# Reordering a seven-product matrix multiplication: even tiles first, half of the sums beside it, weight sums on VectorE

## The chip, the cores and the metric

The kernel runs on one core of a Trainium2 chip. The metric is device time in microseconds (us) of one execution. A profile's span is about 1.7 us shorter than the time of the same run, since it goes from the first to the last instruction. Engines: TensorE (PE; PEld is its weight load), VectorE (DVE), ScalarE (ACT), GpSimd (POOL) and SyncE (SP), which only issues transfers here.

## The reference

```python
# scan: batch 4, heads 8, 768 steps, head_dim 32, state 16, in chunks
y[:, :, sl] = y_intra + y_inter           # decayed scores @ x, and C @ state
# then, on x = y as 3072 x 256:
h = x @ w_in                              # 256 -> 2048
g = h * np.clip(h + 3.0, 0.0, 6.0) / 6.0
return g @ w_out                          # 2048 -> 256
```

## The kernel before

It cuts the 768 steps into six blocks k = 0 to 5 of 128 steps (512 rows over the batch). In each block TensorE makes a first product h (16 tiles f of 128 columns), ScalarE and VectorE turn each tile into gT, and TensorE makes the second product g @ w_out, with the scan of block k + 1 woven between. Block 0 also decodes the weights, which arrive in pieces as 64-bit floats, and uses a plain second product.

```python
r = ffn.tile([P, TB], FP32, name="r", bufs=3)
nc.scalar.activation(r, h, AF.Relu, bias=half, scale=1.0 / 6.0)
nc.vector.scalar_tensor_tensor(
    out=gTs[k][:, f], in0=r, scalar=1.0, in1=h, op0=ALU.min, op1=ALU.mult)
```

From block 1 on the second product uses seven products of quarters instead of eight. Quarters are even and odd tiles (e) by row halves (r); sums of quarters are made by VectorE, four operations for each two pairs of tiles. The sums of w_out's quarters are made once.

```python
js = slice(j0, j0 + 2)
a11, a12, a21, a22 = (g_quarter(k, e, r)[:, js] for r in range(2) for e in range(2))
for o, p_, q_, op in ((s1, a21, a22, ALU.add), (s2, s1, a11, ALU.subtract),
                      (a21, a11, a21, ALU.subtract), (s4, a12, s2, ALU.subtract)):
    nc.vector.tensor_tensor(out=o, in0=p_, in1=q_, op=op)
...                                        # the units, in order, for each row half t:
unit(oa, 1, quarter(1, 0), w4[:, 1, 0])    # odd tiles
unit(oa, 2, total(2), wsums[2])            # a sum
unit(oa, 0, quarter(0, 0), w4[:, 0, 0])    # even tiles
...
SUMS = {5: 0, 9: 2, 13: 4, 15: 6}          # after which tile f which sums are emitted
```

GpSimd masks the decay tiles L of the scan. Block c's masking is emitted at the head of block c - 1, beside which block c's scan runs, but GpSimd's queue runs ahead as far as its waits let it.

```python
def hide(c, b):
    L = Ls[c, b]
    nc.gpsimd.affine_select(
        out=L, in_=L, pattern=[[0, NH], [1, P]], compare_op=ALU.is_ge,
        fill=-1e5, base=0, channel_multiplier=-1)
```

The first products use four PSUM buffers (`ps`, bufs=4), so tile f of h can start when gT of tile f - 4 is done.

Of the kernel before, what the change touches and what calls it, by code (L numbers as in the profile page):

```python
# [2 lines left out]

# [6 lines left out]
FP32 = mybir.dt.float32  # L10
# [4 lines left out]
ALU = mybir.AluOpType  # L15
# [5 lines left out]
def kernel(  # L21
# [23 lines left out]
    nc = tc.nc  # L45
    P = 128
    NB, NH, S, D = x.shape
# [15 lines left out]
    ffn = ctx.enter_context(tc.tile_pool(name="ffn", bufs=1))  # L63
    ps = ctx.enter_context(tc.tile_pool(name="ps", bufs=4, space=PSUM))
    ps_o = ctx.enter_context(tc.tile_pool(name="ps_o", bufs=2, space=PSUM))
# [36 lines left out]
    def load_w(i):  # L102
# [31 lines left out]
        out=head, in_=head, pattern=[[-2 * N, NQ], [-N, 2]], compare_op=ALU.is_ge,  # L134
        fill=0.0, base=0, channel_multiplier=1)
    nc.gpsimd.affine_select(
        out=head, in_=head, pattern=[[2 * N, NQ], [N, 2]], compare_op=ALU.is_ge,
# [3 lines left out]
        out=parity, in_=head.rearrange("p q t -> p t q"), axis=mybir.AxisListType.X,  # L141
        op=ALU.add)


    def decode(i):
# [44 lines left out]
        out=a_sb, in0=a_sb, scalar1=1e-6, scalar2=1.0, op0=ALU.max, op1=ALU.min)  # L190
    nc.scalar.activation(a_sb, a_sb, AF.Ln)
    nc.vector.tensor_tensor_scan(
        out=flat, data0=run.rearrange("g c p -> g (c p)"), data1=a_sb, initial=0.0,
# [6 lines left out]
    def load_decay(c, b):  # L200
        L = big([P, NH, P], "L")
        src = cum_d[c, b * NH:(b + 1) * NH].rearrange("h p -> (h p)").unsqueeze(0)
        nc.sync.dma_start(
            out=L.rearrange("j h i -> j (h i)"), in_=src.to_broadcast([P, NH * P]))
        Ls[c, b] = L

    def load_eto(c):
        eto = att.tile([P, NB, P], FP32, name="eto")
        for h in range(NH):
            nc.sync.dma_start(  # L210
                out=eto[h * N:(h + 1) * N],
                in_=cum_d[c, h:NB * NH:NH].unsqueeze(0).to_broadcast([N, NB, P]))
        etos[c] = eto
# [173 lines left out]
    def mlp_out(k, b, f0, f1):  # L387
        if f0 == 0:
            outs[k, b] = ps_o.tile([P, DM], FP32, name="o", tag="o")
        o = outs[k, b]  # L390
        for f in range(f0, f1):
            nc.tensor.matmul(  # L392
                out=o, lhsT=gTs[k][:, f, b * P:(b + 1) * P], rhs=w_out[:, f],
                start=(f == 0), stop=(f == NF - 1))
        if f1 == NF:
            ob = ffn.tile([P, DM], FP32, name="ob", bufs=3)
            nc.scalar.copy(out=ob, in_=o)
            r0 = b * S + k * P
            nc.sync.dma_start(out=out[r0:r0 + P, :], in_=ob)
# [6 lines left out]
    w4 = w_out.rearrange("p (j e) (m c) -> p e m j c", e=2, m=2)  # L406
    wsums = {}

    def weight_sums():
        t3 = const.tile([P, NJ, P], FP32, name="t3")  # L410
        t2, t4 = (att.tile([P, NJ, P], FP32, name=n, tag="wm") for n in ("t2", "t4"))
        t1 = w4[:, 0, 1]
        for engine, o, p_, q_ in ((nc.vector, t3, w4[:, 1, 1], w4[:, 0, 1]),
                                  (nc.vector, t1, w4[:, 0, 1], w4[:, 0, 0]),
                                  (nc.gpsimd, t2, w4[:, 1, 1], t1),
                                  (nc.gpsimd, t4, w4[:, 1, 0], t2)):
            engine.tensor_tensor(out=o, in0=p_, in1=q_, op=ALU.subtract)
        wsums.update({1: t1, 2: t2, 3: t3, 4: t4})

    gsums, ends_out = {}, {}  # L420

    def g_quarter(k, e, r):
        return gTs[k].rearrange("p (j e) (r i) -> p e r j i", e=2, r=2)[:, e, r]

    def g_sums(k, j0):

        if j0 == 0:
            gsums[k] = {n: loads.tile([P, NJ, 2 * P], FP32, name=f"s{n}", tag="raw", bufs=NRAW)
                        for n in (1, 2, 4)}
        js = slice(j0, j0 + 2)  # L430
        a11, a12, a21, a22 = (g_quarter(k, e, r)[:, js] for r in range(2) for e in range(2))
        s1, s2, s4 = (gsums[k][n][:, js] for n in (1, 2, 4))
        for o, p_, q_, op in ((s1, a21, a22, ALU.add), (s2, s1, a11, ALU.subtract),
                              (a21, a11, a21, ALU.subtract), (s4, a12, s2, ALU.subtract)):
            nc.vector.tensor_tensor(out=o, in0=p_, in1=q_, op=op)  # L435

    def out_units(k, t):

        def quarter(e, r):
            return g_quarter(k, e, r)[:, :, t * P:(t + 1) * P]  # L440

        def total(n):
            return gsums[k][n][:, :, t * P:(t + 1) * P]

        def unit(bank, slot, lhs, rhs):
            for j in range(NJ):
                nc.tensor.matmul(  # L447
                    out=bank[:, slot], lhsT=lhs[:, j], rhs=rhs[:, j],
                    start=(j == 0), stop=(j == NJ - 1), skip_group_check=True)

        oa = ps_o.tile([P, 4, P], FP32, name="oa", tag="o")
        unit(oa, 1, quarter(1, 0), w4[:, 1, 0])
        yield
        unit(oa, 2, total(2), wsums[2])
        yield
        unit(oa, 0, quarter(0, 0), w4[:, 0, 0])
        x1 = ffn.tile([P, P], FP32, name="x1", bufs=2)
        nc.scalar.copy(out=x1, in_=oa[:, 0])  # L458
        res = ffn.tile([P, 5, P], FP32, name="res", bufs=2)
        nc.vector.tensor_tensor(  # L460
            out=res[:, 0:5:4], in0=oa[:, 1:3], in1=x1.unsqueeze(1).to_broadcast([P, 2, P]),
            op=ALU.add)
        yield
        ob = ps_o.tile([P, 4, P], FP32, name="ob", tag="o")
        unit(ob, 2, total(4), w4[:, 1, 1])
        yield
        unit(ob, 3, quarter(1, 1), wsums[4])
        yield
        unit(ob, 0, total(1), wsums[1])
        yield  # L470
        unit(ob, 1, quarter(0, 1), wsums[3])
        u = ffn.tile([P, 2, P], FP32, name="u", bufs=2)
        nc.vector.tensor_tensor(  # L473
            out=u, in0=ob[:, 0:2], in1=res[:, 4:5].to_broadcast([P, 2, P]), op=ALU.add)
        nc.vector.tensor_tensor(out=res[:, 1:3], in0=ob[:, 2:4], in1=u, op=ALU.add)
        nc.vector.tensor_tensor(out=res[:, 3], in0=ob[:, 0], in1=u[:, 1], op=ALU.add)
        for r in range(2):
            r0 = (t + 2 * r) * S + k * P
            nc.sync.dma_start(
                out=out[r0:r0 + P, :], in_=res[:, 2 * r:2 * r + 2].rearrange("p m c -> p (m c)"))  # L480
        yield

    def beside_in(c, f):

# [13 lines left out]
    def beside_out(c, b):  # L498

        if b == 0 and c + 1 < NC:  # L500
            for i in range(NB):
                load_decay(c + 1, i)
            load_eto(c + 1)
        if b in (2, 4):
            mix(c, (b - 2, b - 1))
        if b < NB:
            scores(c, b)
        if b in (2, 4):
            keep(c, b // 2 - 1)

    def load(c):
        load_bc(c)
        load_x(c)
# [3 lines left out]
    def weights(i, n):  # L517
        for _ in range(n):
            next(parts[i], None)
# [36 lines left out]
    for i in range(2, NP + 1):  # L556
        for j in range(5):
            weave.setdefault(4 * i - 7 + j, []).append(i)
    SCAN = {0: 0, 3: 1, 5: 2, 8: 3, 10: 4}
    SUMS = {5: 0, 9: 2, 13: 4, 15: 6}  # L560
    for k in range(NC):
        c = k + 1
        for f in range(NF):
            mlp_in(k, f)
            if k + 2 < NC and f == (0 if k else NF - 1):
                load(k + 2)
            if k == 0:
                for i in weave.get(f, []):
                    weights(i, 1)
            if c < NC:  # L570
                beside_in(c, f)
            if k and f in SUMS:
                g_sums(k, SUMS[f])
        if k == 0:
            weights(NP + 1, 3)
            beside_out(c, 0)
            for i in range(NP):
                for b in range(2):
                    mlp_out(0, b, i * FP, (i + 1) * FP)
                if i + 1 < NP:  # L580
                    weights(NP + i + 1, 2)
                    if i + 2 < NP:
                        weights(NP + i + 2, 3)
                    beside_out(c, i + 1)
            mlp_out(k, 2, 0, NF)
            beside_out(c, 4)
            mlp_out(k, 3, 0, NF)
            weight_sums()
        else:
            units = itertools.chain(out_units(k, 0), out_units(k, 1))  # L590
            for i, _ in enumerate(units):
                if c < NC and i in SCAN:
                    beside_out(c, SCAN[i])

# [29 lines left out]
```

## Time and profile before

| | before |
|---|---|
| median, first runs | 418.98 us (418.66 to 420.82) |
| span of the profile, of a run of 420.41 us | 418.7 us |
| TensorE / VectorE / ScalarE / GpSimd busy | 91 / 53 / 39 / 10% |
| first product of block 1 | 34.73 us |
| the same in block 3, without a gap | 28.35 us |

TensorE is the engine to follow: its row in the timeline, its brackets (idle time just before an instruction, and what ended it) and its granted clock.

### The profile page before, as it was taken

Reading aid. Unit: us, or ns where it says so; the run is one execution under the profiler, and the core shown is the slowest. Engines: PE = TensorE matmul, PEld = TensorE weight load, DVE = VectorE, ACT = ScalarE, POOL = GpSimd, SP = SyncE. Lnnn points to the kernel's source line nnn. Section 1 sums busy time; section 2 is a strip of 40 time slices with the busy share of each in tenths; the row PEclk is TensorE's granted clock in tenths of the full one; section 3 lists DMA queues with packets and bytes.
Section 4 is the critical chain, followed back from the end, with each engine's and each line's share of the span. In section 5 each row is a group of like instructions: output and inputs, shape, how many; then the busy total and the mean of one; then the engine's idle time right before and its main releaser. Section 6 shows DMA issues by size and latency. Waiting matters only on the chain.

```text
span 418.7 us, 6489 instructions
## 1 busy us (share of the span) xinstructions
PE 381.6 (91%) x2588; PEld 261.7 (63%) x2588; DVE 223.9 (53%) x412; ACT 164.0 (39%) x370; POOL 43.7 (10%) x44
## 2 busy tenths in 40 slices
PE   0488788989996999999899999999999999999995
PEld 0253334768642599844499844599844689744895
DVE  5367778951349744138944138934138923266611
ACT  5386999520294300088200088200188200133100
POOL 1326100000574000005000004000000000000000
PEclk9999998999996999999999999999999999999999
DMA  9897966930591000096000096000000000000000
GB/s 157 231 340 233 156 234 131 188 127 21 58 258 24 2 1 28 6 124 222 0 2 27 8 129 217 2 2 27 27 0 0 2 2 26 27 0 0 2 27 25
DMA packets 87614, 32.33 MB, mean 77 GB/s; under 512 B 75584, under 2 KB 81408, under 8 KB 87584
## 3 DMA queue, kind: packets, MB, share of 16 engines
q1 hardware_dynamic: 87584, 31.92, 36.6%
q8 instruction: 20, 0.33, 0.3%
q14 instruction: 10, 0.08, 0.1%
HBM read 28.67 MB, written 3.24 MB: 76 GB/s over the span
## 4 chain that ended last, share of the span: by engine, by line
PE 49%; DVE 17%; ACT 16%; DMA 9%; issue 5%; SPq 1%; POOL 1%; ACTq 0%; DVEq 0%; POOLq 0%
PE ob L447 18%; PE oa L447 12%; PE h L378 10%; ACT L L251 9%; DVE gT L384 5%; DMA bc<-in_C_dram 5%; ACT r L383 5%; DVE s L435 5%; PE o L392 4%; DMA L<-cum_d 3%; PE cb L305 2%; PE y L337 2%; PE y L328 1%; DMA eto<-cum_d 1%; DVE gT L435 1%
## 5 line engine op out<-in xcount | busy, mean ns | idle before, releaser
L378 PE MATMUL h<-yT,w_in 128*128 128x512 f32 x384 | 171.3, 602 | 9.5 <-DVE w_in L182 5.1
L378 PEld LDWEIGHTS h<-yT,w_in 128*128 128x128 f32 x384 | 72.7, 193 | 96.9 <-issue 79.5
L383 ACT ACTIVATE r<-h,half 128x512 f32<-128x512 f32 x96 | 64.5, 684 | 78.4 <-PE h L378 74.2
L384 DVE SCALAR_TENSOR_TENSOR gT<-r,h 128x512 f32<-128x512 f32 x96 | 64.1, 684 | 55.9 <-ACT r L383 55.6
L251 ACT ACTIVATE L<-L,cum_n 128x128 f32<-128x128 f32 x192 | 58.4, 397 | 5.6 <-POOL L L242 5.6
L313 DVE TENSOR_TENSOR L<-L,cb 128x256 f32<-128x256 f32 x96 | 33.9, 416 | 42.1 <-PE cb L305 42.1
L447 PE MATMUL oa<-w_out,gT 128*128 128x128 f32 x320 | 40.7, 278 | 3.2 <-DVE gT L384 3.2
L447 PEld LDWEIGHTS oa<-w_out,gT 128*128 128x128 f32 x320 | 38.1, 192 | 7.8 <-DVE gT L384 4.1
L447 PE MATMUL ob<-t,gT 128*128 128x128 f32 x320 | 40.2, 279 | 0.0
L447 PEld LDWEIGHTS ob<-t,gT 128*128 128x128 f32 x320 | 37.3, 192 | 3.1 <-issue 2.9
L447 PE MATMUL ob<-w_out,s 128*128 128x128 f32 x320 | 39.0, 275 | 0.0
L447 PEld LDWEIGHTS ob<-w_out,s 128*128 128x128 f32 x320 | 37.3, 192 | 0.0
L242 POOL TENSOR_SCALAR_AFFINE_SELECT L<-L 128x1024 f32<-128x1024 f32 x24 | 29.5, 1241 | 44.3 <-DMA L<-cum_d 34.9
L392 PE MATMUL o<-w_out,gT 128*128 128x256 f32 x128 | 30.7, 399 | 2.5 <-DVE w_out L182 2.5
L458 ACT COPY x<-oa 128x128 f32<-128x128 f32 x10 | 2.7, 265 | 76.2 <-PE oa L447 76.2
L392 PEld LDWEIGHTS o<-w_out,gT 128*128 128x128 f32 x128 | 25.1, 199 | 7.6 <-DVE w_out L182 3.3
L305 PE MATMUL cb<-cT,bT 32*128 32x256 f32 x192 | 22.7, 473 | 6.7 <-DVE cT L286 5.6
L360 ACT COPY yT<-y 128x256 f32<-128x256 f32 x24 | 7.7, 374 | 47.3 <-PE y L345 37.0
L473 DVE TENSOR_TENSOR u<-ob,res 128x256 f32<-128x256 f32 x10 | 4.2, 425 | 35.1 <-PE ob L447 35.1
L447 PE MATMUL oa<-t,s 128*128 128x128 f32 x160 | 19.9, 278 | 0.0
L447 PEld LDWEIGHTS oa<-t,s 128*128 128x128 f32 x160 | 18.6, 192 | 1.3 <-issue 1.3
L305 PEld LDWEIGHTS cb<-cT,bT 32*128 32x128 f32 x192 | 10.5, 204 | 12.8 <-DVE cT L286 6.7
(64 smaller groups left out, 252.4 us busy)
## 6 DMA issues: line engine op xcount, KB each, us to landing
L<-cum_d SPq DMA_DIRECT2D x24, 512.0 KB, 7.0
raw<-in_moe_w_in_dram SPq DMA_DIRECT2D x4, 1024.0 KB, 8.4
raw<-in_moe_w_out_dram SPq DMA_DIRECT2D x4, 1024.0 KB, 6.9
xt<-in_x_dram SPq DMA_DIRECT2D x6, 512.0 KB, 8.6
out_dram<-res SPq DMA_DIRECT2D x20, 128.0 KB, 1.8
bc<-in_C_dram SPq DMA_DIRECT2D x6, 256.0 KB, 5.2
bc<-in_B_dram SPq DMA_DIRECT2D x6, 256.0 KB, 7.6
eto<-cum_d SPq DMA_DIRECT2D x40, 32.0 KB, 5.8
```

The lines of the kernel that those rows point to most:

```text
L242: nc.gpsimd.affine_select(out=L, in_=L, pattern=[[0, NH], [1, P]], compare_op=ALU.is_ge, fill=-1e5, base=0, channel_multiplier=-1)
L251: nc.scalar.activation(L[:, h], L[:, h], AF.Exp, bias=cum_n[:, c, g:g + 1])
L305: nc.tensor.matmul(out=cb.rearrange("j h i -> j (h i)"), lhsT=bT[rows, b % 2], rhs=cT[rows, b % 2].rearrange("n t i -> n (t i)"), start=Tr ...
L313: nc.vector.tensor_tensor(out=L[:, hs], in0=L[:, hs], in1=cbs[q], op=ALU.mult)
L337: nc.tensor.matmul(out=y_ps[u][32 * q:32 * q + 32, b % 2], lhsT=xt[:, b * NH + h], rhs=L[:, h], start=(c == 0), stop=True, tile_position=( ...
L360: nc.scalar.copy(out=yTs[c][:, u, bs_], in_=y_ps[u][:, 0:2])
L378: nc.tensor.matmul(out=h, lhsT=w_in[:, j, f * P:(f + 1) * P], rhs=yTs[k][:, j].rearrange("p b i -> p (b i)"), start=(j == 0), stop=(j == N ...
L383: nc.scalar.activation(r, h, AF.Relu, bias=half, scale=1.0 / 6.0)
L384: nc.vector.scalar_tensor_tensor(out=gTs[k][:, f], in0=r, scalar=1.0, in1=h, op0=ALU.min, op1=ALU.mult)
L392: nc.tensor.matmul(out=o, lhsT=gTs[k][:, f, b * P:(b + 1) * P], rhs=w_out[:, f], start=(f == 0), stop=(f == NF - 1))
L435: nc.vector.tensor_tensor(out=o, in0=p_, in1=q_, op=op)
L447: nc.tensor.matmul(out=bank[:, slot], lhsT=lhs[:, j], rhs=rhs[:, j], start=(j == 0), stop=(j == NJ - 1), skip_group_check=True)
```

## The change

Four parts. The units are reordered so that the first four of a block need no sums. The third group of g's sums moves from tile 13 to after tile 15, where the fourth already was, so that half of the sums run beside the second product; the first two groups move from tiles 5 and 9 to 6 and 10. Three of the scan's pieces between units come one unit later (SCAN). One unit product of each row half (x1) is copied for both at once. The four weight sums, two of which were on GpSimd, all go to VectorE, three of them inside block 0. The intent is that TensorE goes from first to second product without a wait.

```diff
-        t1 = w4[:, 0, 1]
-        for engine, o, p_, q_ in ((nc.vector, t3, w4[:, 1, 1], w4[:, 0, 1]),
-                                  (nc.vector, t1, w4[:, 0, 1], w4[:, 0, 0]),
-                                  (nc.gpsimd, t2, w4[:, 1, 1], t1),
-                                  (nc.gpsimd, t4, w4[:, 1, 0], t2)):
+        for o, p_, q_, op in ((t3, w4[:, 1, 1], w4[:, 0, 1], ALU.subtract),
+                              (t2, t3, w4[:, 0, 0], ALU.add),
+                              (t4, w4[:, 1, 0], t2, ALU.subtract)):
+            nc.vector.tensor_tensor(out=o, in0=p_, in1=q_, op=op)
...
+            if t == 0:
+                unit(oa, 0, quarter(0, 0, 0), w4[:, 0, 0])      # even tiles, both halves
+                yield
+                unit(oa, 3, quarter(0, 0, 1), w4[:, 0, 0])
+                yield
+            unit(oa, 1, quarter(1, 0, t), w4[:, 1, 0])          # odd tiles
...
+            unit(ob, 3, quarter(1, 1, t), wsums[4])             # a plain quarter
+            yield
+            unit(oa, 2, total(2, t), wsums[2])                  # the first sum
...
-    SCAN = {0: 0, 3: 1, 5: 2, 8: 3, 10: 4}
-    SUMS = {5: 0, 9: 2, 13: 4, 15: 6}
+    SCAN = {1: 0, 4: 1, 6: 2, 8: 3, 10: 4}
+    SUMS = {6: (0,), 10: (2,), 15: (4, 6)}
...
+                if k == 1 and f == 1:
+                    weight_sum_in_place()
```

More of the change, by code (lines that the diff above doesn't have):

```diff
@@ L1 @@
-import itertools
 from contextlib import ExitStack
@@ L411, in weight_sums, with weight_sum_in_place @@
         t2, t4 = (att.tile([P, NJ, P], FP32, name=n, tag="wm") for n in ("t2", "t4"))
-        t1 = w4[:, 0, 1]
-        for engine, o, p_, q_ in ((nc.vector, t3, w4[:, 1, 1], w4[:, 0, 1]),
-                                  (nc.vector, t1, w4[:, 0, 1], w4[:, 0, 0]),
-                                  (nc.gpsimd, t2, w4[:, 1, 1], t1),
-                                  (nc.gpsimd, t4, w4[:, 1, 0], t2)):
-            engine.tensor_tensor(out=o, in0=p_, in1=q_, op=ALU.subtract)
-        wsums.update({1: t1, 2: t2, 3: t3, 4: t4})
-    gsums, ends_out = {}, {}
+        for o, p_, q_, op in ((t3, w4[:, 1, 1], w4[:, 0, 1], ALU.subtract),
+                              (t2, t3, w4[:, 0, 0], ALU.add),
+                              (t4, w4[:, 1, 0], t2, ALU.subtract)):
+            nc.vector.tensor_tensor(out=o, in0=p_, in1=q_, op=op)
+        wsums.update({1: w4[:, 0, 1], 2: t2, 3: t3, 4: t4})
+    def weight_sum_in_place():
+        nc.vector.tensor_tensor(
+            out=w4[:, 0, 1], in0=w4[:, 0, 1], in1=w4[:, 0, 0], op=ALU.subtract)
+    gsums = {}
     def g_quarter(k, e, r):
@@ L435, in g_sums, with out_units, quarter, total @@
             nc.vector.tensor_tensor(out=o, in0=p_, in1=q_, op=op)
-    def out_units(k, t):
-        def quarter(e, r):
+    def out_units(k):
+        def quarter(e, r, t):
             return g_quarter(k, e, r)[:, :, t * P:(t + 1) * P]
-        def total(n):
+        def total(n, t):
             return gsums[k][n][:, :, t * P:(t + 1) * P]
@@ L449, in unit @@
                     start=(j == 0), stop=(j == NJ - 1), skip_group_check=True)
-        oa = ps_o.tile([P, 4, P], FP32, name="oa", tag="o")
-        unit(oa, 1, quarter(1, 0), w4[:, 1, 0])
-        yield
-        unit(oa, 2, total(2), wsums[2])
-        yield
-        unit(oa, 0, quarter(0, 0), w4[:, 0, 0])
-        x1 = ffn.tile([P, P], FP32, name="x1", bufs=2)
-        nc.scalar.copy(out=x1, in_=oa[:, 0])
-        res = ffn.tile([P, 5, P], FP32, name="res", bufs=2)
-        nc.vector.tensor_tensor(
-            out=res[:, 0:5:4], in0=oa[:, 1:3], in1=x1.unsqueeze(1).to_broadcast([P, 2, P]),
-            op=ALU.add)
@@ L463, in out_units @@
-        yield
-        ob = ps_o.tile([P, 4, P], FP32, name="ob", tag="o")
-        unit(ob, 2, total(4), w4[:, 1, 1])
-        yield
-        unit(ob, 3, quarter(1, 1), wsums[4])
-        yield
-        unit(ob, 0, total(1), wsums[1])
-        yield
-        unit(ob, 1, quarter(0, 1), wsums[3])
-        u = ffn.tile([P, 2, P], FP32, name="u", bufs=2)
-        nc.vector.tensor_tensor(
-            out=u, in0=ob[:, 0:2], in1=res[:, 4:5].to_broadcast([P, 2, P]), op=ALU.add)
-        nc.vector.tensor_tensor(out=res[:, 1:3], in0=ob[:, 2:4], in1=u, op=ALU.add)
@@ L476, in out_units @@
-        nc.vector.tensor_tensor(out=res[:, 3], in0=ob[:, 0], in1=u[:, 1], op=ALU.add)
-        for r in range(2):
-            r0 = (t + 2 * r) * S + k * P
-            nc.sync.dma_start(
-                out=out[r0:r0 + P, :], in_=res[:, 2 * r:2 * r + 2].rearrange("p m c -> p (m c)"))
-        yield
+        for t in range(2):
+            oa = ps_o.tile([P, 4, P], FP32, name="oa", tag="o")
+            if t == 0:
[4 more added lines that the diff above has]
+            unit(oa, 1, quarter(1, 0, t), w4[:, 1, 0])
+            if t == 0:
+                x1 = ffn.tile([P, 2, P], FP32, name="x1")
+                nc.scalar.copy(out=x1, in_=oa[:, 0:4:3])
+            yield
+            ob = ps_o.tile([P, 4, P], FP32, name="ob", tag="o")
+            unit(ob, 3, quarter(1, 1, t), wsums[4])
+            yield
+            unit(oa, 2, total(2, t), wsums[2])
+            res = ffn.tile([P, 5, P], FP32, name="res", bufs=2)
+            nc.vector.tensor_tensor(
+                out=res[:, 0:5:4], in0=oa[:, 1:3],
+                in1=x1[:, t:t + 1].to_broadcast([P, 2, P]), op=ALU.add)
+            yield
+            unit(ob, 2, total(4, t), w4[:, 1, 1])
+            yield
+            unit(ob, 0, total(1, t), wsums[1])
+            yield
+            unit(ob, 1, quarter(0, 1, t), wsums[3])
+            u = ffn.tile([P, 2, P], FP32, name="u", bufs=2)
+            nc.vector.tensor_tensor(
+                out=u, in0=ob[:, 0:2], in1=res[:, 4:5].to_broadcast([P, 2, P]), op=ALU.add)
+            nc.vector.tensor_tensor(out=res[:, 1:3], in0=ob[:, 2:4], in1=u, op=ALU.add)
+            nc.vector.tensor_tensor(out=res[:, 3], in0=ob[:, 0], in1=u[:, 1], op=ALU.add)
+            for r in range(2):
+                r0 = (t + 2 * r) * S + k * P
+                nc.sync.dma_start(
+                    out=out[r0:r0 + P, :],
+                    in_=res[:, 2 * r:2 * r + 2].rearrange("p m c -> p (m c)"))
+            yield
@@ L571 @@
                 beside_in(c, f)
-            if k and f in SUMS:
-                g_sums(k, SUMS[f])
+            if k:
+                if k == 1 and f == 1:
+                    weight_sum_in_place()
+                for j0 in SUMS.get(f, ()):
+                    g_sums(k, j0)
         if k == 0:
@@ L586 @@
             beside_out(c, 4)
+            weight_sums()
             mlp_out(k, 3, 0, NF)
-            weight_sums()
         else:
-            units = itertools.chain(out_units(k, 0), out_units(k, 1))
-            for i, _ in enumerate(units):
+            for i, _ in enumerate(out_units(k)):
                 if c < NC and i in SCAN:
```

## The prediction

> **What bounds the kernel now.** I read the page's busy shares and slices first, then TensorE's own timeline for its gaps, then the timeline of all engines around each gap, and last a table of stretches for the granted clock.
>
> ```profile
> PE 381.6 (91%) x2588; PEld 261.7 (63%) x2588; DVE 223.9 (53%) x412; ACT 164.0 (39%) x370; POOL 43.7 (10%) x44
> ...
> PEclk9999998999996999999999999999999999999999
> ```
>
> TensorE sets the pace from about 100 us on: work is taken from it or added to it only through its gaps and its clock (one slice of 10.5 us, the thirteenth, has 0.6). The change leaves the number of matmuls alone, so only gaps count. A block k = 1 to 5 is a first product (64 matmuls of h at 0.43 us, plus two groups of transposes) and a second one (14 units of 16 matmuls at 0.112 us, 1.79 us each, with the scan's pieces between). With no gap the first product takes 28.35 us, as in block 3 (238.59 to 266.94).
>
> ```profile
> 204.92 1.73 PE L447 MATMUL oa<-w_out,gT 128*128 128x128 f32 x14
> 207.83 0.49 PE L447 MATMUL oa<-w_out,gT 128*128 128x128 f32 x2 [1.19 <-DVE gT L384]
> ...
> 269.71 0.49 PE L447 MATMUL oa<-w_out,gT 128*128 128x128 f32 x2 [1.04 <-DVE gT L384]
> ...
> 331.01 0.49 PE L447 MATMUL oa<-w_out,gT 128*128 128x128 f32 x2 [0.46 <-DVE gT L384]
> ```
>
> First kind of gap: the second product starts with a unit of odd tiles, whose last two matmuls need tile 15 of gT, which VectorE makes behind eight or more sums. The bracket understates the loss, since a busy matmul's end is modelled; from start to start, 14 matmuls should take 1.56 us and took 2.91 (block 2), 2.77 (3), 2.19 (4) and 1.96 (1 and 5). The loss is 1.35 + 1.21 + 0.63 + 0.40 + 0.40 = 3.99 us.
>
> ```profile
> 122.81 5.57 POOL L242 TENSOR_SCALAR_AFFINE_SELECT L<-L 128x1024 f32<-128x1024 f32 x4 [2.76 <-PE t_ps L280]
> 123.00 1.45 DVE L435 TENSOR_TENSOR s<-gT 128x512 f32<-128x512 f32 x1
> ...
> 127.35 1.57 DVE L435 TENSOR_TENSOR s<-gT,s 128x512 f32<-128x512 f32 x1
> ...
> 128.85 1.27 DVE L384 SCALAR_TENSOR_TENSOR gT<-r,h 128x512 f32<-128x512 f32 x2
> ...
> 129.57 6.41 PE L378 MATMUL h<-yT,w_in 128*128 128x512 f32 x8 [3.42 <-DVE gT L384]
> ```
>
> Second kind, in block 1 alone: the first four sums (emitted after tile 5) took 5.85 us beside GpSimd's masking of L, against 2.5 us in block 2 (from 189.42 on). Tile 6 of gT waited behind them, its PSUM bank stayed full, and TensorE stood still 3.42 us. Then its clock fell:
>
> ```profile
> 126.00:129.00 3.00, 0.16 (x1) 0.00 (x0) 3.00 (x3) 3.00 (x10) 2.98 (x3) 0.87 0.21 39
> 129.00:132.00 3.00, 2.42 (x3) 1.17 (x4) 3.00 (x6) 0.70 (x2) 0.84 (x1) 0.50 0.00 0
> 132.00:135.00 3.00, 3.00 (x5) 1.14 (x4) 2.97 (x6) 0.69 (x1) 0.00 (x0) 0.50 0.00 0
> ```
>
> (Columns: stretch, its length, PE, PEld, DVE, ACT and POOL busy, PEclk, DMA share, GB/s.) Eight matmuls of h took 6.41 us instead of 3.5. Block 1's first product ran from 108.39 to 143.12, 34.73 us: 6.38 lost. Block 2's lost 0.73 (29.08 us), the same wait in small.
>
> [...] a sum of two SBUF tensors took 1.45 to 1.57 us beside GpSimd and 0.69 alone, while gT, with one input in PSUM, stayed at 0.69. [...] the trace has 2.36 us on GpSimd and 1.22 on VectorE for one weight sum. [...] another drop (0.55 in 70 to 72 us) followed 66.3 to 70.0 us, where 0.64 us of score matmuls ran. A gap of 2.2 us before 50.33 caused none.
>
> **The change, part by part.**
>
> *Order of units.* The first two units now read untouched even tiles, the third and fourth odd tiles and a plain quarter; the fifth is the first that reads sums. Tile 15 is needed only in the third unit, 2 × 1.79 + 0.65 (scores) + 1.56 = 5.8 us into the product, where gT 15 is ready 1.6 us after the last h (r 0.69, gT 0.69 and latency). The 3.99 us go, unless a later wait replaces them.
>
> *Half of the sums beside the product.* Eight sums follow tile 15: 8 × 0.69 = 5.5 us. Block 2 by hand: h ends at 204.3, gT 15 at 206.15, the last s2 at 210.3, the last sum at 211.65. The fifth unit starts at 204.3 + 4 × 1.79 + 0.65 = 212.1, needing s2 near its end. Block 5, without scores, starts it 7.15 us after h; s2 is there 5.5 us after h. No wait. The scores' multiplications follow at 213.1, before the next scores at 213.9. x1 is copied once for both halves; nothing waits on it.
>
> *Sums after tiles 6 and 10 in place of 5 and 9.* The gT tile that TensorE wants next now comes before the sums. Block 2's 0.73 us go: h 15 needs gT 11 by 202.5, and I get 201.8. In block 1 the masking is started by its transfer (122.81), which nothing here moves, and the sums start at 122.6, so they collide again. They end near 128.45, gT 7 at 129.1; h 11 could have started at 127.7. So about 1.45 us of standing remains[...]. Block 1's first product takes 28.35 + 1.45 = 29.8 us and gains 4.9.
>
> *Weight sums.* GpSimd's 2 × 2.36 us go, VectorE gets two more of 1.22. Three sit at 102.5 to 106.1, where VectorE was idle; the one in place sits after gT 1 at 113.4 and delays gT 2 by 0.2 us, inside four banks of slack. ScalarE's wait of 0.91 us for the masking in block 1 goes as well; that is counted above, as I took ScalarE's times from block 2.
>
> *What GpSimd now does earlier.* Its queue no longer waits for the weight sum at 108 us before masking block 2's L. Those loads are issued at 74.84 and land 5.9 to 8.2 us later, so four maskings of 1.1 us run at about 83 to 88.5 us, on top of VectorE's last decoding, which TensorE awaits:
>
> ```profile
> 36.89 1.57 DVE L171 TENSOR_TENSOR we<-we,ws 128x1024 uint16<-128x1024 uint16 x1
> ...
> 86.99 0.69 DVE L171 TENSOR_TENSOR we<-we,ws 128x1024 uint16<-128x1024 uint16 x1
> 87.71 1.22 DVE L182 SCALAR_TENSOR_TENSOR w_out<-wm,we 128x1024 f32<-128x1024 f32 x1
> ...
> 88.99 10.63 PE L392 MATMUL o<-w_out,gT 128*128 128x256 f32 x48 [1.91 <-DVE w_out L182]
> ```
>
> The first line is that operation beside an earlier masking: 1.57 against 0.69 us. The two others went from 1.22 to 1.46 and 1.50. With a partial overlap, up to 0.24 + 0.88 + 0.28 = 1.4 us; I take 1.2, all on the path. The gap before 88.99 becomes about 3.1 us with 0.64 us of scores ahead of it, like the stretch before 70 us. I give a clock drop 55%[...].
>
> **Sum.** Gained: 3.99 + 0.73 + 4.9 = 9.6 us. Lost: 1.2 + 0.9 = 2.1 us. 418.98 - 7.5 = 411.5 us, 1.8% faster.
>
> **Rivals.**
> 1. *The wait moves to the sums*: the fifth unit waits for s2, or the scores for a bank behind eight sums. For it: only 0.8 us of slack to the second scores. Against: every duration used is measured with VectorE uncontended there. If VectorE runs 1.5 us later, each of four blocks loses up to 0.7 us: 414.
> 2. *The masking still stops TensorE in block 1 long enough for the clock to drop.* For it: the overlap is nearly the same as before. Against: one tile more is ahead of the sums, worth 1.72 us of h. With it, 3 us come back: 414.5.
> 3. *Block 0 pays nothing*: the maskings fall between VectorE's two-input SBUF operations[...], or land early. Then 409.4 us.
> 4. *TensorE hides it all anyway*, the gains being modelled gaps only. Against: starts, not ends, were used. It would be 417.
>
> **Range and chances.** Without the clock drop in block 0 the sum is 410.6, with it 412.3; the boundary of 2% is 410.6. Rivals 1 and 2 push up, 3 down. Range 408.8 to 414.5; faster by over 2% 0.41, within 2% 0.57, slower 0.02.
>
> **What would show it.** Right: no gap ahead of the second product's third unit in blocks 1 to 5; first products of 28.4 us in blocks 2 to 4 and near 30 in block 1, with no clock below 0.9 there; maskings at 83 to 89 us, with L171 of block 0 longer than 0.69 us there and the last 48 matmuls of o starting near 90.2 after a gap near 3 us. Wrong: a wait of oa or ob on the sums, a clock of 0.5 near 130 us, or o starting at 89.0 as before.

Cuts are marked in this text, and in three expectations below, where they told of the hardware what no trace or run of this case shows. The sum stands: 9.6 us gained and 2.1 lost, so 7.5 us. The loss of 0.9 us was worked out: 55% of 1.7 us, the author's figure for one drop of the clock in block 0, which also lies between 410.6 and 412.3. The profile before shows such a drop: at a clock of 0.53 (70.0 to 73.4 us) 16 matmuls of o took 5.41 us, and 3.72 at 76.59, 1.7 us less. The 1.45 us left in block 1 should bring no drop; that was the author's estimate.

## The result, and the profile after

The changed kernel took 413.51 us (413.22 to 413.84) against 419.8 us (418.66 to 420.82) of the kernel before in the same rounds; ratio 0.9851, interval 0.9818 to 0.9884. Ratios are the mean time of one kernel's fast runs over that of the other's of the same rounds, so not quite the ratio of the medians. It is 1.5% faster.

Cutting both profiles at the same instructions of TensorE (the start of the last 48 matmuls of o, of each first h, of each first oa) gives the whole difference:

| stretch of TensorE | before | after | measured | predicted |
|---|---|---|---|---|
| start to the last 48 matmuls of o | 88.99 | 91.12 | +2.1 | +1.2 |
| those and the rest of block 0 | 19.40 | 21.09 | +1.7 | +0.9 (1.7 at 55%) |
| block 1, first product | 34.73 | 28.99 | -5.7 | -4.9 |
| block 2, first product | 29.08 | 28.35 | -0.7 | -0.7 |
| blocks 3 to 5, first products | 84.17 | 84.17 | 0 | 0 |
| five second products, with the end | 162.33 | 157.88 | -4.5 | -4.0 |
| span | 418.7 | 411.6 | -7.1 | -7.5 |

The page's rows of the profile after, and TensorE around the start of two second products (columns: start, busy, engine, line, operation; xN is merged instructions):

```profile
PE 378.7 (92%) x2588; PEld 261.3 (63%) x2588; DVE 227.3 (55%) x414; ACT 163.0 (40%) x365; POOL 40.4 (10%) x42
...
PEclk9999989998999999999999999999999999999999
```

```profile
201.77 3.73 PE L450 MATMUL oa<-w_out,gT 128*128 128x128 f32 x32
205.44 0.71 PE L304 MATMUL cb<-cT,bT 32*128 32x256 f32 x8
206.08 2.05 PE L450 MATMUL oa<-w_out,gT 128*128 128x128 f32 x16
207.97 1.95 PE L450 MATMUL ob<-t,gT 128*128 128x128 f32 x16
209.75 1.95 PE L450 MATMUL oa<-t,s 128*128 128x128 f32 x16
...
382.16 5.52 PE L450 MATMUL oa<-w_out,gT 128*128 128x128 f32 x48
```

There is no bracket left: each unit starts 1.78 us after the one before it, or 1.89 (206.08 to 207.97) where scan work has just run. The waits on gT are gone and none on a sum took their place. The busy share of PE hardly moved; the gaps did.

Block 1 in the profile after, all engines, and its clock (stretch, length, PE, PEld, DVE, ACT, POOL busy, PEclk, DMA share, GB/s):

```profile
126.20 4.08 POOL L241 TENSOR_SCALAR_AFFINE_SELECT L<-L 128x1024 f32<-128x1024 f32 x3 [3.77 <-PE h L377]
126.39 1.45 DVE L437 TENSOR_TENSOR s<-gT 128x512 f32<-128x512 f32 x1
...
130.75 0.68 DVE L437 TENSOR_TENSOR s<-gT,s 128x512 f32<-128x512 f32 x1
...
132.07 1.98 PE L377 MATMUL h<-yT,w_in 128*128 128x512 f32 x4 [0.38 <-DVE gT L383]
```

```profile
129.00:132.00 3.00, 2.69 (x7) 0.91 (x5) 3.00 (x5) 3.00 (x10) 2.30 (x2) 1.00 0.45 98
```

Masking and sums still meet, but TensorE stops for 0.38 us and not 3.42, and the clock stays at 1.00.

What the change cost is in block 0. VectorE and GpSimd there:

```profile
85.86 1.22 DVE L169 SCALAR_TENSOR_TENSOR wm<-raw,wm 128x1024 f32<-128x1024 uint32 x1
```

That was the first of the three decoding operations before; after, with GpSimd:

```profile
82.76 3.75 POOL L241 TENSOR_SCALAR_AFFINE_SELECT L<-L 128x1024 f32<-128x1024 f32 x3 [33.97 <-DMA L<-cum_d]
...
85.47 2.11 DVE L168 SCALAR_TENSOR_TENSOR wm<-raw,wm 128x1024 f32<-128x1024 uint32 x1
...
86.91 1.62 POOL L241 TENSOR_SCALAR_AFFINE_SELECT L<-L 128x1024 f32<-128x1024 f32 x1 [0.40 <-PE cb L304]
87.50 1.57 DVE L170 TENSOR_TENSOR we<-we,ws 128x1024 uint16<-128x1024 uint16 x1
88.50 1.49 POOL L261 TENSOR_TENSOR bs<-bc,e_from 128x512 f32<-128x512 f32 x1
89.11 1.96 DVE L181 SCALAR_TENSOR_TENSOR w_out<-wm,we 128x1024 f32<-128x1024 f32 x1
...
91.12 12.31 PE L391 MATMUL o<-w_out,gT 128*128 128x256 f32 x48 [4.42 <-DVE w_out L181]
```

```profile
92.50:96.00 3.50, 3.50 (x12) 2.85 (x11) 0.00 (x0) 0.37 (x1) 0.00 (x0) 0.61 0.10 37
```

The three decoding operations took 2.11, 1.57 and 1.96 us; the same three took 1.22, 0.69 and 1.22 before, so 2.5 us are lost (the profile after had started 0.4 us earlier, which makes the table's +2.1). The gap grew from 1.91 to 4.42 us, the clock fell to 0.61 in the next stretch, and the 48 matmuls took 12.31 us instead of 10.63.

The end times of these lines fit two engines that take turns. The third masking ends at 82.76 + 3.75 = 86.51 and L168 ends 1.07 us later; the fourth masking ends at 88.53, 0.95 us after that; L170 at 89.07, 0.54 us later; bs at 89.99, 0.92 later; L181 at 91.07, 1.08 later. Each is that operation's own duration (1.22, 1.09, 0.69, 1.06, 1.22) less 0.14 or 0.15 us. So none of the five need have been slowed: each fits a wait until the other engine's instruction has ended. The prediction had not seen that.

### The profile page after: what moved, and what is told of

It is laid out like the page before. It is cut to its first block, busy times and chain, and to the rows that moved or that the text cites. A ratio compares the mean times of both kernels' runs of the same rounds, so it can differ in the third digit from the quotient of the medians.

```text
span 411.6 us, 6492 instructions
## 1 busy us (share of the span) xinstructions
PE 378.7 (92%) x2588; PEld 261.3 (63%) x2588; DVE 227.3 (55%) x414; ACT 163.0 (40%) x365; POOL 40.4 (10%) x42
## 4 chain that ended last, share of the span: by engine, by line
PE 74%; DMA 9%; ACT 5%; issue 4%; DVE 4%; SPq 1%; POOL 1%; POOLq 0%; DVEq 0%; ACTq 0%
PE h L377 29%; PE ob L450 18%; PE oa L450 13%; PE o L391 6%; DMA L<-cum_d 5%; ACT L L250 3%; PE cb L304 3%; DMA bc<-in_C_dram 2%; PE y L336 2%; PE y L327 1%; DVE gT L383 1%; DMA eto<-cum_d 1%; ACT r L382 1%; POOL L L241 1%; SPq L202 1%
## 5 line engine op out<-in xcount | busy, mean ns | idle before, releaser
L382 ACT ACTIVATE r<-h,half 128x512 f32<-128x512 f32 x96 | 64.5, 685 | 73.4 <-PE h L377 70.3
L450 PEld LDWEIGHTS oa<-w_out,gT 128*128 128x128 f32 x320 | 37.2, 192 | 3.7 <-issue 3.7
L241 POOL TENSOR_SCALAR_AFFINE_SELECT L<-L 128x1024 f32<-128x1024 f32 x24 | 31.2, 1309 | 78.7 <-DMA L<-cum_d 67.6
L450 PE MATMUL oa<-w_out,gT 128*128 128x128 f32 x320 | 38.4, 276 | 0.0
L304 PEld LDWEIGHTS cb<-cT,bT 32*128 32x128 f32 x192 | 10.5, 203 | 12.6 <-DVE cT L285 6.5
L471 DVE TENSOR_TENSOR res<-oa,x 128x256 f32<-128x256 f32 x10 | 4.2, 425 | 24.4 <-PE oa L450 15.8
```

The source lines that it names most:

```text
L241: nc.gpsimd.affine_select(out=L, in_=L, pattern=[[0, NH], [1, P]], compare_op=ALU.is_ge, fill=-1e5, base=0, channel_multiplier=-1)
L304: nc.tensor.matmul(out=cb.rearrange("j h i -> j (h i)"), lhsT=bT[rows, b % 2], rhs=cT[rows, b % 2].rearrange("n t i -> n (t i)"), start=Tr ...
L450: nc.tensor.matmul(out=bank[:, slot], lhsT=lhs[:, j], rhs=rhs[:, j], start=(j == 0), stop=(j == NJ - 1), skip_group_check=True)
L471: nc.vector.tensor_tensor(out=res[:, 0:5:4], in0=oa[:, 1:3], in1=x1[:, t:t + 1].to_broadcast([P, 2, P]), op=ALU.add)
```

## The experiments

| run | median us (lowest to highest) | ratio to before (95%) |
|---|---|---|
| maskings after the decoding | 408.39 (408.31 to 410.32) | 0.9769 (0.9731 to 0.9806) |
| gap filled | 411.70 (410.30 to 412.24) | 0.9833 (0.9796 to 0.9870) |
| two sums back on GpSimd | 409.23 (408.80 to 411.00) | 0.9788 (0.9750 to 0.9825) |
| all maskings later | 408.67 (407.98 to 410.56) | 0.9773 (0.9735 to 0.9811) |
| third group of sums inside | 415.61 (413.62 to 416.61) | 0.9929 (0.9895 to 0.9963) |
| old order of units | 420.57 (419.53 to 421.62) | 1.0053 (1.0022 to 1.0084) |
| sums at 5 and 9 | 414.03 (411.50 to 415.98) | 0.9891 (0.9854 to 0.9929) |
| weight sums alone | 419.89 (416.32 to 420.81) | 1.0011 (0.9965 to 1.0056) |
| maskings later, gaps filled | 408.52 (407.30 to 408.73) | 0.9753 (0.9724 to 0.9781) |
| changed kernel again | 413.08 (411.13 to 414.21) | 0.9861 (0.9829 to 0.9893) |
| before, maskings later | 412.84 (412.62 to 414.33) | 0.9867 (0.9835 to 0.9900) |

The first four, the next four and the last three each shared the runs of the kernel before (medians 418.23, 418.69 and 418.56 us). All results were correct. Where a run of another group is set against the changed kernel's 413.08 us, the difference is one of medians. Worked out from the ratios, the gain of the first four is smaller by 0.2 to 0.8 us, and the loss of the next group larger by 0.3.

### Block 0: what the early maskings cost

**Maskings after the decoding.** One tiny operation at the head of GpSimd's queue makes it wait for the last decoded piece:

```diff
+        if c == 2 and b == 0:
+            gate = const.tile([P, 1], FP32, name="gate")
+            last = w_out[:, NF - 1, 0:1]
+            nc.gpsimd.tensor_tensor(out=gate, in0=last, in1=last, op=ALU.subtract)
         nc.gpsimd.affine_select(
```

> The changed kernel plus one tiny GpSimd operation that reads the last decoded piece of w_out, ahead of the four maskings of block 2, so that they start after VectorE's decoding and not on top of it. Theory (GpSimd's early masking stretches three VectorE operations by 0.89 + 0.88 + 0.74 = 2.5 us[...]): the three operations are back at 1.22, 0.69 and 1.22 us, the last 48 matmuls of o take 10.6 us, and the time falls by 4.2 us to about 409.3. Rival (the decoding is late for another reason, say a transfer): no change, 413.5.

```profile
84.20 1.22 DVE L168 SCALAR_TENSOR_TENSOR wm<-raw,wm 128x1024 f32<-128x1024 uint32 x1
...
87.33 10.63 PE L395 MATMUL o<-w_out,gT 128*128 128x256 f32 x48 [1.91 <-DVE w_out L181]
...
87.52 4.22 POOL L245 TENSOR_SCALAR_AFFINE_SELECT L<-L 128x1024 f32<-128x1024 f32 x4
```

The theory holds: 408.39 us, 4.7 below the changed kernel's 413.08 (3.9 by the ratios; 4.2 were expected, the 2.5 and the 1.7 us by which the 48 matmuls' 12.31 us exceed 10.63). Four maskings take 4.22 us here, undisturbed. (This profile's first h began 1.2 us earlier than the changed kernel's, before any of this.)

**Two sums back on GpSimd.** An undoing of one part, with the same aim by another way:

```diff
-        for o, p_, q_, op in ((t3, w4[:, 1, 1], w4[:, 0, 1], ALU.subtract),
-                              (t2, t3, w4[:, 0, 0], ALU.add),
-                              (t4, w4[:, 1, 0], t2, ALU.subtract)):
+        for engine, ... in ((nc.vector, t3, ...), (nc.gpsimd, t2, ...), (nc.gpsimd, t4, ...)):
```

> The changed kernel with two of its three weight sums of block 0 given back to GpSimd (undoing that part only). GpSimd's queue then waits at the first of them until about 104 us, so the maskings of block 2 fall behind it as before. Theory: the collision in block 0 goes, 409.3 like the run with the small operation ahead of the maskings. Rival (the sums on GpSimd cost something in block 1, by delaying the maskings or by contention): 410 to 412.

409.23 us. So the weight sums' place costs the changed kernel 3 to 4 us, not by their own work but by no longer holding back GpSimd's queue.

**The gap filled.** Only the clock is treated; the collision stays:

```diff
+                if i == NP - 1:
+                    idle = ps_y.tile([P, 4, P], FP32, name="y0")
+                    for _ in range(4):
+                        nc.tensor.matmul(out=idle..., lhsT=w_in[:, 0, 0:P], rhs=yTs[0][:, 0]...)
```

> The changed kernel with four needless matmuls (8 rows of 0.43 us, 3.4 us in all, into a PSUM bank that nobody reads) in TensorE's gap before the last 48 matmuls of o. The maskings still collide with the decoding. Theory (of the 4.2 us lost in block 0, 2.5 are the late decoding and 1.7 the clock that the idle gap halves): o still starts near 91.1, but runs its 48 matmuls in 10.6 us and not 12.3; 411.8. Rival (the slow o is not from the gap, or the clock drops anyway): 413.5.

```profile
91.24 10.52 PE L391 MATMUL o<-w_out,gT 128*128 128x256 f32 x48
```

o starts as late as in the changed kernel and runs at full clock: 411.70 us, 1.4 below the changed kernel's 413.08. The intervals of the two ratios overlap, so the times alone would not show it; the 10.52 us do, and so does the clock: 1.00 from 92.5 to 96 us, where it was 0.61. The idle gap is what lowered it.

It isn't only long gaps. Over twelve profiles, the 48 matmuls took 12.31 us after each of the five gaps of 3.56 us or more (the changed kernel twice, sums at 5 and 9, third group inside, weight sums alone), 10.5 to 10.6 in the two filled ones, and 10.63 after four of the gaps of 1.91 us besides that of the kernel before; but with the two sums back on GpSimd the profile caught this:

```profile
88.71 12.31 PE L391 MATMUL o<-w_out,gT 128*128 128x256 f32 x48 [1.91 <-DVE w_out L181]
```

That run was its kernel's slowest, 411.00 us. Nor is a drop after such a gap rare elsewhere. In block 0's first product six of the thirteen profiles have 16 matmuls of h at 8.83 us instead of 7.13, after gaps of 1.78 to 2.25 us, the changed kernel in both of its profiles; here the second:

```profile
50.01 8.83 PE L377 MATMUL h<-yT,w_in 128*128 128x512 f32 x16 [1.78 <-DVE w_in L181]
```

In the other profiles gaps of 1.78 to 2.22 us at these places did nothing. So after a gap of about 2 us the next matmuls took 1.7 us longer in some profiles and not in others, and no single profile can show that a gap is short enough.

### The second product: order or sums?

**Old order of units**, the kernel before with only the new places of the sums:

```diff
-    SUMS = {5: 0, 9: 2, 13: 4, 15: 6}
+    SUMS = {6: (0,), 10: (2,), 15: (4, 6)}
```

> The kernel before with only the new places of the sums (after tiles 6, 10, and two groups after 15), its order of units and its weight sums kept. Theory: the second unit now waits for eight sums after tile 15, about 1.8 us lost per block against none in the changed kernel, 9 us in five blocks in place of 4; blocks 1 and 2 gain about 5 + 0.7 us in their first products; together about 419, no gain. Rival (the places of the sums carry the gain by themselves): 414 or below.

```profile
206.22 0.71 PE L447 MATMUL oa<-t,s 128*128 128x128 f32 x4 [1.19 <-DVE s L435]
...
391.58 0.86 PE L447 MATMUL oa<-t,s 128*128 128x128 f32 x4 [1.82 <-DVE s L435]
```

420.57 us, slightly slower than before: the second unit waits for the sums in all five blocks. In block 5, after the wait of 1.82 us, the unit behind it took 3.47 us instead of 1.95. Moving the sums without the order is worse than nothing.

**Third group of sums inside**, the changed kernel with one group moved back:

```diff
-    SUMS = {6: (0,), 10: (2,), 15: (4, 6)}
+    SUMS = {6: (0,), 10: (2,), 13: (4,), 15: (6,)}
```

> The changed kernel with its third group of sums back inside the first product (after tile 13; the fourth stays after tile 15), so only the order of units and the two early groups' places remain changed. Theory (the order of units alone removes the gap at the start of the second product; tile 15 has over 3 us to spare): same as the changed kernel within 0.5 us, 413.5. Rival (making half of the sums beside the product is what removes the gap): each of five blocks loses 0.4 to 1 us, 415.5 to 418.

```profile
141.69 2.27 PE L450 MATMUL oa<-w_out,gT 128*128 128x128 f32 x18 [0.25 <-DVE gT L383]
...
203.33 2.27 PE L450 MATMUL oa<-w_out,gT 128*128 128x128 f32 x18 [0.80 <-DVE gT L383]
```

The theory falls: 415.61 us, 2.5 slower than the changed kernel. With sums after tile 13, the even tile 14 comes late for the very first unit. The order of units needs the half of the sums out of its way, and the sums need the order. The profile is of this kernel's fastest run and accounts for a net 1.2 us in blocks 1 to 5; the other 1.3 of the medians stay open.

### Block 1: what stopped TensorE

**Before, maskings later.** The kernel before with GpSimd's maskings for blocks c = 3 to 5 held until the last sum of g of block c - 2, the block in which they would otherwise run early (the same tiny operation, for c >= 3, reading the last tile of sums).

> The kernel before with one thing altered: the maskings of blocks 3 to 5 wait for the last sum of g of the block before. Theory (the overlap of maskings and sums made TensorE's 3.42 us stop in block 1, and the stop made the clock drop): the first sums take 0.7 us each, no stop over 0.5 us and no drop near 130 us, first product of block 1 near 29 us, and block 2's 0.7 us gone: 412 to 413. Rival (ScalarE's late start in block 1 makes the stop): 417 or more.

```profile
122.56 0.69 DVE L439 TENSOR_TENSOR s<-gT 128x512 f32<-128x512 f32 x1
123.28 0.69 DVE L439 TENSOR_TENSOR s<-s,gT 128x512 f32<-128x512 f32 x1
...
122.14 7.39 PE L382 MATMUL h<-yT,w_in 128*128 128x512 f32 x16
```

412.84 us. Tiles 8 to 11 of h run through in 7.39 us (7.03 without any wait), with no drop of the clock near 130 us (the next 16, from 129.80, take 7.03). So the meeting of maskings and sums made the stop, and this one tiny operation alone is worth as much as the whole change.

**Sums at 5 and 9**, the changed kernel with `SUMS = {5: (0,), 9: (2,), 15: (4, 6)}`:

> The changed kernel with its two early groups of sums after tiles 5 and 9, as before. Theory: block 2's 0.7 us of standing return, and in block 1 the sums again hold up the tile that TensorE wants next: about 1.3 us more without a clock drop, together 415.5[...]. Rival (ScalarE's earlier start, or something else, cured block 1): 413.5 to 414.

414.03 us, nearer to the rival's number than to the theory's. The trace has 0.48 us more in block 1 and 0.61 in block 2, no clock drop near block 1's sums (after a stop of 0.86 us eight matmuls of h take 3.70 us): half of what the theory expected. With the weight sums off GpSimd, the sums' places are worth 0.5 us in block 1 and are not what kept its clock up in this profile.

**Weight sums alone**, the kernel before with only the changed kernel's weight sums:

> The kernel before with only the new weight sums (three on VectorE in block 0, the fourth in place in block 1). Theory: it loses in block 0 what the changed kernel loses there, 2.5 us and mostly 1.7 us more of a halved clock, and keeps block 1's stop: about 4 us slower than before, 423.5. Rival (the weight sums on GpSimd were what delayed block 1): faster than before, 417 or below.

```profile
126.13 0.69 DVE L437 TENSOR_TENSOR s<-gT 128x512 f32<-128x512 f32 x1
126.85 1.53 DVE L437 TENSOR_TENSOR s<-s,gT 128x512 f32<-128x512 f32 x1
...
132.02 3.27 PE L378 MATMUL h<-yT,w_in 128*128 128x512 f32 x7 [1.70 <-DVE gT L384]
```

419.89 us, the theory's 423.5 missed and the rival's 417 as well; but the runs are widely spread, two of six at 416.3 and 416.9, and the profile is of one of 420.35. Both things are in the trace. Block 1 starts at 112.56 us instead of 108.39, 4.2 lost as in the changed kernel; and block 1 takes 63.02 us instead of 67.45, 4.4 gained. With GpSimd free of weight sums ScalarE no longer waits for a masking (0.91 us in the kernel before), the sums start 1.0 us earlier (13.57 us after the block's start, 14.61 before), the first of them is done before the masking begins, TensorE stops 1.70 us and its clock stays up (the next eight matmuls of h take 3.70 us, and 6.41 in the kernel before). Either part does it alone: with the earlier start here block 1's first product takes 30.31 us, with other places of the sums in the old-order run, which stops 1.73 us, 30.34, against 34.73 before, and 28.99 with both. That these two stops brought no drop of the clock is from one profile each; after stops of 1.78 and 1.82 us elsewhere 16 matmuls of h took 8.83 us for 7.13, and a unit 3.47 for 1.95.

### Versions that beat both kernels

**All maskings later**: the tiny operation also ahead of the maskings of blocks 3 to 5.

> As the run that delays the maskings of block 2, and in addition the maskings of blocks 3 to 5 wait for the last sum of g of the block before, so that they meet no sums. Theory: block 1's remaining stop (0.6 us in its first product) goes as well: 0.6 us below the run with only block 2's maskings delayed, about 408.7, and no VectorE sum longer than 0.7 us after 100 us. Rival (maskings that late hold up ScalarE's exponentials of the next block): slower than that run.

Block 1's whole length falls to 60.56 us, equal to blocks 2 and 3. But 408.67 us is no better than 408.39 with block 2's maskings alone; the 0.6 us expected are below the spread of these runs, and not shown.

**Maskings later, gaps filled**: needless matmuls in six gaps of block 0.

```diff
+    def fill(n):
+        idle = ps_y.tile([P, 4, P], FP32, name="y0")
+        for _ in range(n): ...                              # as in the gap filled above
+    FILL = {4: 1, 8: 2, 12: 1}                              # ahead of these tiles of h
...
+                if i in (1, 3):
+                    fill(2)                                 # ahead of these pieces of o
```

> The kernel with all maskings of blocks 2 to 5 delayed, and needless matmuls in TensorE's gaps of block 0 (one or two, 0.86 us each, ahead of h 4, 8 and 12, of the first scores, and of the second and last pieces of o). Theory (each profile so far shows one or two clock drops of 1.7 us in block 0[...]): no clock below 0.97 after 35 us, 1.7 to 3.4 us less than 408.7, so 405.3 to 407. Rival (the drops are not from the gaps, or the needless matmuls delay the needed ones by as much): 408.7 or more.

No slice of the clock row is below 9 tenths any more (0.998 in the mean), yet 408.52 us: the time is near the rival's, but for neither of its reasons. The drops were from the gaps, since they went with them (7.13 us for every 16 matmuls of h in block 0, 3.72 for each of the first three 16 of o, 10.63 for the 48), and the needed matmuls were not delayed. Why nothing was gained is seen by comparing the run with all maskings later,

```profile
69.68 5.41 PE L395 MATMUL o<-w_out,gT 128*128 128x256 f32 x16
...
76.31 3.72 PE L395 MATMUL o<-w_out,gT 128*128 128x256 f32 x16 [0.58 <-DVE w_out L181]
```

with this one,

```profile
69.54 3.72 PE L395 MATMUL o<-w_out,gT 128*128 128x256 f32 x16
...
76.19 3.72 PE L395 MATMUL o<-w_out,gT 128*128 128x256 f32 x16 [0.38 <-DVE w_out L181]
```

The first piece of o lost 1.7 us to the clock there, and the second started only 0.1 us later, since it waits for VectorE's decoding either way. In block 0 a slow clock cost time where TensorE was the one waited for, after the last decoding (12.31 us for 10.63), and next to none here. The filled version has the narrower spread of the two, 1.4 us against 2.6.

**Changed kernel again**, as a common measure:

> The changed kernel itself once more, in the same rounds as the two others, as a common measure. 412.5 to 413.8; a profile with the last 48 matmuls of o at 12.3 us after a gap over 3.5 us.

413.08 us, the gap 3.56 us and the 48 matmuls 12.31. In this run L168 began 0.1 us ahead of a masking and took 1.22 us: it was the masking that waited (it and the next took 3.56 us; a masking alone takes 1.09 in the kernel before). So the loss in block 0 varies with who comes first.

## Why the prediction was right

The forecast was 411.5 us, 1.8% faster; measured 413.5 and, again, 413.1 (1.5 and 1.4%). Both are in the range, and the likeliest class, within 2%, is the one that came. That the sum came so close (-7.5 forecast, -7.1 by the spans) is in part luck: block 0 lost 3.8 us where 2.1 were forecast, and block 1 and the second products gained 1.3 more than forecast. The forecast also took gains read from a profile of a run of 420.41 us off a median of 418.98.

- *Order of units, with half of the sums beside.* Right: 4.0 us expected, 4.5 found, and no wait on a sum. The other 0.1 us per block is in the two matmuls that had waited: in block 5 of the kernel before they took 0.32 us from start to start (390.75 to 391.07) and not 0.22. That the sums' place is part of it, the prediction had not said; the run with the third group inside showed it.
- *Block 2's 0.7 us.* Right.
- *Block 1.* Right in kind, 4.9 against 5.7. The sums took 4.96 us (126.39 to 131.35) and not 5.85, because the fourth masking came 0.7 us late, its wait put down to a transfer, and let the last sum pass alone. But the step credited the sums' new places. The runs credit the weight sums' leaving GpSimd as much: each alone gained 4.4 us in the first product, and beside the other the new places were worth 0.5.
- *Weight sums on VectorE.* Right: they filled idle time, and the one in place stopped nothing.
- *Block 0.* The mechanism was right, and the size off. The term "up to 0.24 + 0.88 + 0.28 = 1.4 us; I take 1.2" measured 0.89 + 0.88 + 0.74 = 2.5 us. The prediction read earlier stretched durations as a slowdown in proportion to the overlap. The end times fit turn-taking: each of three operations ended its own duration less 0.14 or 0.15 us after a GpSimd instruction, the third after bs, which I had left out.
- *The clock in block 0.* The 55% case came: the 1.7 us put down for it measured 1.68 (12.31 less 10.63). With the longer gap it was likelier than I made it, five profiles of five. But "a gap of 2.2 us before 50.33 caused none" was one profile's luck: after the change the gap of 2.16 us at that place was followed by 8.83 us instead of 7.13. It cost next to nothing there: the next group of h began at 59.03 us, and at 59.24 before, where it had waited for VectorE's decoding.
- *Rivals.* 1 and 4 are refuted by the trace, 2 did not come, 3 (block 0 pays nothing) was made real by delaying the maskings, and gave 408.4 where it said 409.4.

## What to carry to other kernels

When work leaves a queue, ask what in that queue it was holding back: here two sums on GpSimd had kept four maskings off VectorE's critical operations, and one tiny operation that waits for the right moment bought about 4 us. Where decoding operations of VectorE met GpSimd's instructions here, each overlap fitted a wait for the other's instruction to end: 2.5 us on three operations, where an estimate in proportion to the overlap had given 1.2. And judge a gap of TensorE together with the clock after it, but only where TensorE is what the rest waits for: here 1.7 us of slow clock moved the next piece of o by 0.1 us, since that piece waited for VectorE's decoding.
